# Half of the first Wq load issued from a second DMA queue

**The chip, the cores, the metric.** One core of one Trainium2 chip. The metric is the device time of one call in microseconds (us), lower is better.

## The reference

Four residual blocks on x of 2048 rows by 1024 columns in bf16: attention, feed-forward, attention, feed-forward, with the same weights in both rounds. Each block first normalises its input by rows. Only the first step of the first block matters here: the layer norm of the first 512 rows, and the Q projection of them.

```python
def _A_ref(x, wqkv, wo):              # x is normalised, wqkv is [1024, 3072]
    qkv = x @ wqkv                    # -> q, k, v, 32 heads of 32
    ...                               # 8 dilated positions (step 2) per row, softmax
    return o @ wo
x = x + _A_ref(_layernorm(x), A_wqkv, A_wo)
x = x + _B_ref(_layernorm(x), B_w1, B_b1, B_w2, B_b2)
...                                   # both once more
```

## The kernel before

The kernel works on groups of 512 rows (four tiles of 128 rows, x0 to x3 in the first group). `act`, `vec`, `pool` and `sp` wrap ScalarE, VectorE, GpSimd and SyncE; `.on = True` keeps the instructions of that engine in program order. All loads at the start are issued by SyncE: two x tiles, then 512 KB of Wq (two row blocks of 128 rows, of eight) in turn with the other x tiles.

```python
def load_wq_piece(wt, k):
    sp.dma_start(wt[:, k % (KD // 2):k % (KD // 2) + 2, :], wqkv_v[:, k:k + 2, 0:D])

load_x(0, 0, 2)                                   # x0, x1
wq_first = [wpool.tile([P, KD // 2, D], BF16, name="wt") for _ in range(2)]
for k in range(0, KD, 2):                         # KD = 8
    load_wq_piece(wq_first[k // (KD // 2)], k)
    if k < 4:
        load_x(0, 2 + k // 2, 3 + k // 2)         # x2, x3
...
act.activation(one[:], eps_t[:], ACT.Sqrt)        # brings in the Sqrt table early
```

Meanwhile TensorE runs 14 warm-up matmuls. VectorE takes the statistics of x0 and x1, ScalarE their square roots (`std`), VectorE normalises both; then TensorE transposes them and starts on Q, two row blocks of Wq at a time, for these two tiles. The transposes of x2 and x3 come in between.

```python
stats(0); stats(1)                                # bn_stats x2, bn_aggr; act: Sqrt -> std
xn0 = norm(0); xn1 = norm(1, (0, 2 * P, D))       # reciprocal, (x - mean) * rstd
transpose_on_pe(xn0, ...); transpose_on_pe(xn1, ...)
stats(2); stats(3)
for tt in range(2, 4):
    first_late.append((norm(tt), xa[0][:, tt, :, :]))
...
for kq in range(4):                               # two row blocks of Wq
    for c in range(7):
        first[c] = qkv_chunk(wq, c, xnT, first.get(c), kq * 2, (kq + 1) * 2, 0, 2)
        if (kq, c) in ((2, 3), (3, 4)):
            transpose_on_pe(*first_late.pop(0), ...)   # x2, then x3
```

The lines L92 and L117 of the profile are the helpers that record the operations and the matmuls; L211 (L213 to L218 in the variants) is the transpose.

## Time and profile before

| | before |
|---|---|
| median of 3 runs | 1230.35 us (1230.22 to 1230.75) |
| profiled span | 1228.4 us |
| TensorE busy | 1221.6 us, 99% |
| x0 landed / statistics of x1 start | 3.43 / 4.90 us |
| first weight load of Wq | 8.23 us |

After 8.23 us TensorE has just one gap, a short one, so a delay of that moment, or a new gap after it, can hardly be made up, and a load can win something only by bringing it forward. The prediction shows the lines of the start.

### The profile page before, as it was taken

The numbers are of one execution on the slowest core, as the hardware profiler recorded it, in microseconds if no ns is written. First come the engines' busy times: TensorE is split into PE (matmuls) and PEld (weight loads), VectorE is DVE, ScalarE is ACT, GpSimd is POOL, SyncE is SP. The second block draws the span as 40 slices with busy tenths as digits, with TensorE's granted clock in tenths as the row PEclk, the third lists the DMA queues.
The fourth block names the chain that finished last, engine by engine and source line by source line (L and its number), as shares of the span: only waits on it lengthen the run. The fifth ranks groups of instructions, "written<-read, shape, count | busy, mean of one in ns | idle before, by whom it ended". The sixth has DMA issues, their size and how long they took to land.

```text
span 1228.4 us, 13955 instructions
## 1 busy us (share of the span) xinstructions
PE 1221.6 (99%) x5720; PEld 632.7 (52%) x5770; DVE 861.5 (70%) x912; ACT 315.6 (26%) x497; POOL 120.9 (10%) x219
## 2 busy tenths in 40 slices
PE   9999999999999999999999999999999999999998
PEld 7666544456444564446544465444654444444444
DVE  7999896998898999375993759937599797011001
ACT  5343253014310233202431024410244001300310
POOL 2330025010101101100001000000000002000000
PEclk9999999999999999999999999999999999999999
DMA  9965674766638645856557565576664558446441
GB/s 302 290 206 164 176 233 151 202 178 199 219 128 245 188 150 166 239 170 175 161 158 230 172 171 181 157 216 201 171 200 147 186 194 209 149 159 194 156 135 52
DMA packets 223647, 226.64 MB, mean 185 GB/s; under 512 B 71824, under 2 KB 190752, under 8 KB 221536
## 3 DMA queue, kind: packets, MB, share of 16 engines
q1 hardware_dynamic: 214704, 208.69, 56.3%
q0 software_dynamic: 8880, 17.07, 4.2%
q8 instruction: 45, 0.74, 0.2%
q14 instruction: 18, 0.15, 0.0%
HBM read 189.01 MB, written 4.19 MB: 157 GB/s over the span
## 4 chain that ended last, share of the span: by engine, by line
PE 99%; DVE 0%; issue 0%; DMA 0%
PE acc L117 99%; DMA x<-in_A_x_dram 0%; DVE stats L92 0%; PE acc L211 0%; DVE xn L92 0%; DVE x L92 0%; DVE mv L92 0%; DVE rstd L92 0%
## 5 line engine op out<-in xcount | busy, mean ns | idle before, releaser
L117 PE MATMUL acc<-xnT,wt 128*128 128x512 bf16 (+1 forms) x3392 | 720.3, 375 | 0.1
L117 PEld LDWEIGHTS <-wt 128*128 128x128 bf16 x3392 | 400.8, 120 | 317.4
L117 PE MATMUL acc<-wt,hT 128*128 128x512 bf16 (+1 forms) x1780 | 386.0, 376 | 2.1
L117 PEld LDWEIGHTS <-hT 128*128 128x128 bf16 x1820 | 178.1, 98 | 209.0
L92 DVE TENSOR_TENSOR big<-big 128x1024 bf16<-128x1024 bf16 (+2 forms) x184 | 244.8, 1359 | 2.2
L92 ACT ACTIVATE hT<-acc,b1T 128x512 bf16<-128x512 f32 x224 | 152.1, 687 | 325.9 <-PE acc L117 325.8
L92 DVE TENSOR_TENSOR big<-qT,kT 128x4096 bf16<-128x4096 bf16 x64 | 143.8, 2283 | 36.3 <-ACT kT L92 35.9
L92 DVE TENSOR_TENSOR big<-abc,vT 128x4096 bf16<-128x4096 bf16 x64 | 144.6, 2284 | 11.0 <-DMA abc<-a 7.1
L92 DVE TENSOR_TENSOR tmp<-acc,b2bc 128x512 f32<-128x512 f32 x56 | 38.6, 689 | 159.8 <-PE acc L117 156.7
L92 ACT CAST qT<-acc 128x512 bf16<-128x512 f32 (+1 forms) x72 | 38.0, 543 | 276.8 <-PE acc L117 274.6
L117 PE MATMUL acc<-wt,oT 128*128 128x512 bf16 x440 | 97.6, 379 | 0.4
L92 DVE BATCH_NORM_STATS2 stats<-x 128x6 f32<-128x512 bf16 x116 | 77.4, 681 | 6.0 <-DMA x<-in_A_x_dram 5.0
L117 PEld LDWEIGHTS <-oT 128*128 128x128 bf16 x448 | 43.8, 98 | 53.0 <-issue 0.3
L92 DVE TENSOR_TENSOR x<-acc,big 128x512 bf16<-128x512 f32 (+1 forms) x9 | 5.7, 632 | 90.0 <-PE acc L117 90.0
L92 POOL TENSOR_TENSOR rstd<-mv,eps_t 128x1 f32<-128x1 f32 x54 | 16.7, 308 | 524.2 <-DVE mv L92 524.2
L92 ACT CAST vT<-acc 128x512 bf16<-128x512 f32 x64 | 37.4, 585 | 101.9 <-PE acc L117 101.9
L92 ACT CAST kT<-acc 128x512 bf16<-128x512 f32 x64 | 37.3, 584 | 64.5 <-PE acc L117 64.5
L92 DVE TENSOR_TENSOR x<-acc,x 128x512 bf16<-128x512 f32 x64 | 42.9, 670 | 5.1 <-PE acc L117 4.7
L92 DVE TENSOR_SCALAR xn<-x,mv,rstd 128x1024 bf16<-128x1024 bf16 (+2 forms) x53 | 28.5, 540 | 20.1 <-POOL rstd L92 19.9
L92 DVE TENSOR_TENSOR x<-tmp,x 128x512 bf16<-128x512 f32 x56 | 38.6, 689 | 1.4
L92 POOL DMA_DIRECT2D big<-big x24 | 13.3, 563 | 212.5 <-DVE big L92 212.5
L92 ACT ACT_TABLE_LOAD x17 | 21.8, 1283 | 38.9 <-DVE e L92 30.5
(62 smaller groups left out, 285.4 us busy)
## 6 DMA issues: line engine op xcount, KB each, us to landing
wt<-in_B_w_dram SPq DMA_DIRECT2D x56, 1024.0 KB, 5.6
wt<-in_B_w_dram SPq DMA_DIRECT2D x64, 896.0 KB, 4.8
wt<-in_A_wqkv_dram SPq DMA_DIRECT2D x46, 1024.0 KB, 5.6
wt<-in_A_wo_dram SPq DMA_DIRECT2D x16, 1024.0 KB, 5.0
abc<-a POOLq DMA_DIRECT2D x32, 256.0 KB, 4.6
big<-big POOLq DMA_DIRECT2D x24, 256.0 KB, 3.8
x<-in_A_x_dram SPq DMA_DIRECT2D x16, 256.0 KB, 7.1
out_dram<-x SPq DMA_DIRECT2D x31, 128.0 KB, 1.8
```

The costliest lines, as they stand in the source:

```text
L92: inst = f(*args, **kwargs)
L117: return pe(nc.tensor.matmul(*args, **kwargs))
```

## The change

The idea: ScalarE has little to do in the first microseconds and has a DMA queue of its own. Let it issue every second row block of the first Wq (1, 3, 5, 7), in pieces of 256 KB, while SyncE issues the others between the x tiles. Two issuers get the loads out sooner, and smaller pieces let the first matmul start on less.

```diff
-    def load_wq_piece(wt, k):
-        sp.dma_start(wt[:, k % (KD // 2):k % (KD // 2) + 2, :], wqkv_v[:, k:k + 2, 0:D])
+    def load_wq_piece(wt, k, engine):
+        engine.dma_start(wt[:, k % (KD // 2), :], wqkv_v[:, k, 0:D])
...
-        load_wq_piece(wq_first[k // (KD // 2)], k)
+        load_wq_piece(wq_first[k // (KD // 2)], k, sp)
...
+    act.on = True
     act.activation(one[:], eps_t[:], ACT.Sqrt)
+    act.on = True
+    for k in range(1, KD, 2):
+        load_wq_piece(wq_first[k // (KD // 2)], k, act)
+    act.on = False
```

## The prediction

> **What bounds the kernel now.** I first read the head of the page and its summary of the chain that ended last.
>
> ```profile
> span 1228.4 us, 13955 instructions
> PE 1221.6 (99%) x5720; PEld 632.7 (52%) x5770; DVE 861.5 (70%) x912; ACT 315.6 (26%) x497; POOL 120.9 (10%) x219
> PE 99%; DVE 0%; issue 0%; DMA 0%
> ```
>
> TensorE is busy for 1221.6 of 1228.4 us and is 99% of the chain. (The timed median, 1230.35 us, is 1.95 us above this span.) The change touches only loads issued in the first 10 us, so I next took the chain for the first 20 us (start, length, what ran):
>
> ```profile
> 0.74 2.69 DMA x<-in_A_x_dram
> 3.46 1.30 DVE stats L92 x2
> ...
> 6.44 0.55 DVE xn L92
> ...
> 7.10 0.74 DVE xn L92 x2
> ...
> 7.89 0.51 PE acc L211 x6
> 8.40 4.01 PE acc L117 x36
> 12.41 0.45 PE acc L211 x8
> 12.85 1.75 PE acc L117 x16
> 14.61 0.45 PE acc L211 x8
> 15.05 5.03 PE acc L117 x46
> ```
>
> No Wq load is in it. The end hangs on x0's landing (3.43 us), then on VectorE's statistics and normalising of tiles 0 and 1 up to 7.84, then on TensorE without a break. L211 are transposes, L117 the matmuls; before 7 us TensorE only runs warm-up matmuls. The timeline of the same stretch (start, length, engine, what, count) shows the work that could break that row:
>
> ```profile
> 4.90 1.23 DVE L92 BATCH_NORM_STATS2 stats<-x 128x6 f32<-128x512 bf16 x2
> 8.03 1.28 DVE L92 BATCH_NORM_STATS2 stats<-x 128x6 f32<-128x512 bf16 x2
> 8.23 3.94 PEld L117 LDWEIGHTS <-wt 128*128 128x128 bf16 x36
> 9.93 1.29 DVE L92 BATCH_NORM_STATS2 stats<-x 128x6 f32<-128x512 bf16 x2 [0.38 <-DMA x<-in_A_x_dram]
> 11.53 0.55 DVE L92 TENSOR_SCALAR xn<-x,mv,rstd 128x1024 bf16<-128x1024 bf16 x1
> 12.14 0.54 PEld L211 LDWEIGHTS <-xn 128*128 128x128 bf16 x8
> ```
>
> These rows are the statistics of x1, x2 and x3, the normalising of x2 and its transposes. The statistics of x3 waited 0.38 us for their DMA, and x2 is normalised after them: done at 11.53 + 0.55 = 12.08, and TensorE needs it at 12.14. Slack: 0.06 us.
>
> The last view is the table of stretches of 1 us; its last two columns are the DMA engines' busy share and GB/s:
>
> ```profile
> 2.00:3.00 1.00, 1.00 (x4) 0.30 (x2) 0.00 (x0) 0.23 (x2) 0.00 (x0) 1.00 0.96 274
> 4.00:5.00 1.00, 1.00 (x4) 0.41 (x3) 0.97 (x4) 0.00 (x0) 0.00 (x0) 1.00 1.02 233
> 6.00:7.00 1.00, 1.00 (x3) 0.15 (x1) 0.93 (x5) 0.29 (x1) 0.00 (x0) 1.00 1.05 387
> ```
>
> The engines are full from 2 us on, at 233 to 300 GB/s up to 6 us and 370 to 400 after it. Bytes arrive in a fixed stream, so what counts is their order.
>
> I checked order against arrival. Summing the stretches gives 0.32 MB moved by 3 us, 0.62 by 4, 0.85 by 5, 1.12 by 6, 1.50 by 7, 1.87 by 8, 2.25 by 9, 2.65 by 10, 3.05 by 11, 3.44 by 12. The DMA view of single issues gives the landings, as issue plus time to landing: x0 3.4, x1 about 4.3, Wq blocks 0-1 7.3 (1.66 + 5.6), x2 7.9 (2.13 + 5.8), blocks 2-3 9.2, x3 9.9 (3.11 + 6.8), blocks 4-5 11.2, blocks 6-7 12.6. In issue order each is complete in the byte count at 2.8, 3.7, 5.8, 6.5, 7.9, 8.6, 9.9 and 11.2 us. So a tile lands 0.6 us (the first two) or about 1.35 us (the others) after the stream has passed it. That rule carries the estimate below.
>
> When TensorE needs Wq: 36 weight loads in 3.94 us are 0.109 us each, 14 for two row blocks. Blocks 0-1 are needed at 8.23, 2-3 at 9.76, 4-5 at 11.29, and 6-7, after the transposes of x2, at about 13.3. Slacks before: 1.0, 0.5, 0.1 and 0.7 us. The start is loaded just in time.
>
> **What the Trainium skill says.** "DMA: Bandwidth & Descriptors", section "Issuing engines are not separate DMA queues": DMAs from scalar, sync or gpsimd run on the same 16 engines and interleave; a second issuer saves only sequencer time. The trace agrees as far as it goes: the engines are already 84 to 100% busy from SyncE's queue alone. The same page, "Queues, rings and completion order": SP and ACT own one queue row each, and every DMA engine takes turns between the rows by packets. The trace before has just one hardware queue carrying data, so it shows nothing of this. "Perfetto Trace Analysis", section "DMA Instruction — HWDGE (DVE, Sync)": the descriptor generator is locked by one sequencer at a time and the profiled length of an issue holds that wait. The first six of SyncE's issues take 0.40 to 0.47 us for either 256 or 512 KB, so ScalarE's issues may be stretched when both want it.
>
> **The change part by part.** The build order of the changed kernel leaves the work of TensorE, VectorE and GpSimd alone.
>
> Removed: nothing in bytes. Four loads of 512 KB become eight of 256 KB, four on each issuer.
>
> Added on ScalarE: four issues right after the Sqrt that ends at 2.24 us (2.04 + 0.20). At 0.45 us each that is 1.8 us, 3.6 if both issuers alternate for the generator. The fourth also waits for x0's landing at 3.43, because the build has only eight DMA semaphores. ScalarE's next work, the first std, started at 5.02 and is needed by VectorE at 6.30, after 0.29 us of run time. Issues that end by 4.1 to 5.9 us cost nothing.
>
> Moved on SyncE: through the same eight semaphores, x3's issue now waits for x1's landing (4.3 to 4.8 us, was issued at 3.11), block 4 for block 1, block 6 for block 0. These waits are mostly hidden behind a full stream.
>
> Moved in the stream: SyncE's row holds x0, x1, block 0, x2, block 2, x3, then 4 and 6; ScalarE's holds 1, 3, 5, 7. x0's first data came about 1 us after its issue, so ScalarE's row begins at about 3.25 us, with 0.40 MB gone. I let both rows share evenly from there and keep the old rate. A tile whose place in SyncE's row ends at s MB is then passed when 0.40 + 2 (s - 0.40) MB have moved, until ScalarE's 1.05 MB are out. x1 (0.52) lands at 4.8, needed at 4.90: just in time. Block 0 (0.79): 1.18 MB, 6.2 + 1.35 = 7.5, fine. x2 (1.05): 1.70 MB, 7.5 + 1.35 = 8.9, wanted at 8.03. Block 2 (1.31): 2.23 MB, 8.9 + 1.35 = 10.3, wanted at 9.76. x3 (1.57): all of ScalarE's row lies before it, 2.62 MB instead of 2.10, 9.9 + 1.35 = 11.3, was 9.91. Block 4: 11.9, wanted at 11.3.
>
> The stalls share one clock and do not add up: block 2 holds TensorE for 0.5 us, block 4 then for about 0.1, and x2's normalising, 2.15 us after the start of x3's statistics (9.93 to 12.08), ends at 13.4 instead of 12.08. TensorE would be at its transposes at 12.8, so the total loss is about 1.3 us. With TensorE full to the end, all of it reaches the end. This is the pessimistic sum: it takes the slow early rate and an even split. If ScalarE's issues come later, or two rows lift the 233 to 300 GB/s, x3 comes back to 10 us and the loss to 0. At 390 GB/s from 3.25 us on, 2.62 MB are passed at 3.25 + 2.22 / 0.39 = 8.9 rather than 9.9, and x3 lands at 10.3: a loss of 0.3 us. I take 0.75 us, near the middle of 0.3 and 1.3: 1231.1 us.
>
> **The rivals.** First, faster streaming through finer pieces and two rows. For it: the slow stretch coincides with SyncE's long run of issues, and 256 KB pieces release TensorE a block at a time. Against it: the engines are counted full there, and no Wq wait is on the chain, so a perfect stream wins only the 0.06 us and perhaps some of the 0.3 us gap inside the first transposes. It would give 1230.1 to 1230.4. Second, ScalarE held up: if its issues block past 6 us, the first std delays normalising, and every 0.1 us passes to the end; at 1 us an issue the fourth ends at 6.3 and costs about 0.3 us, 1230.7 alone. Third, x1 crowded out by ScalarE's first block: it has 0.5 us of room, and I expect it to use that; beyond it, each tenth counts in full. All three rivals and a bad x3 together would make some 1232.3.
>
> **Range and chances.** Low: no loss and 0.25 us of run-to-run spread (the three runs before span 0.5), 1230.1. High: the full x3 loss with 0.6 us of the second or third rival, 1232.3. A step of 2% is 24.6 us, longer than the whole stretch touched: faster 0.5%, within 2% 98.5%, slower 1%.
>
> **What would show it.** Right: in the profile after, a second hardware queue or ScalarE issues of 256 KB from about 2.24 us; x3's statistics starting at 10.3 to 11.3 us with a longer DMA wait; the transposes of x2 starting at 12.5 to 13.5 behind a TensorE gap; the matmul row shifted by the same amount to the end. Wrong: those transposes still at 12.14 with the same span (the rivals of a better stream), or a first real transpose later than 7.05 (ScalarE or x1). An effect over 2 us, or any difference arising after 20 us, would show that I have misread what bounds the start.

## The result

| | before | changed |
|---|---|---|
| median | 1230.30 us (5 runs, 1230.14 to 1230.75) | 1230.67 us (5 runs, 1230.62 to 1231.06) |
| profiled span | 1228.4 us | 1228.9 us |
| statistics of x1 start | 4.90 us | 5.30 us |
| first weight load of Wq | 8.23 us | 8.68 us |

The ratio is 1.0003, with a 95% interval of 0.999 to 1.0017: the same at 2%, and by the interval not even clear of nothing. What makes 0.4 us readable at all is that the profiles show where TensorE falls behind and catches up, and that the same pattern came back in a second set of runs (e6 below).

The head of the page of the changed kernel and, from its table of DMA queues (packets, MB, share of 16 engines), the new hardware queue:

```profile
span 1228.9 us, 14009 instructions
PE 1224.0 (100%) x5770; PEld 632.7 (51%) x5770; DVE 861.9 (70%) x912; ACT 315.8 (26%) x497; POOL 124.4 (10%) x219
...
q10 hardware_dynamic: 576, 1.05, 0.2%
```

The second queue is there: 1.05 MB, which is the four blocks. TensorE's 2.4 us more of busy time is a matter of records: 5770 matmuls against 5720 before, where 50 records were missing (the weight loads are 5770 in both).

The chain that ended last, of the changed kernel's first 20 us (start, length, what):

```profile
1.19 4.08 DMA x<-in_A_x_dram
...
5.30 1.30 DVE stats L92 x2
...
7.54 0.75 DVE xn L92 x2
...
8.34 0.51 PE acc L216 x6
8.85 3.99 PE acc L117 x36
...
15.48 4.59 PE acc L117 x42
```

Set this beside the chain before. There it began with x0, issued at 0.74; here it begins with x1, issued at 1.19 and 4.08 us under way. Before, x1 needed 3.1 us, was there at 4.3 and was not on the chain. From x1 on, the two chains have the same steps of the same length, 0.44 to 0.45 us apart (7.10 and 7.54, 7.89 and 8.34, 8.40 and 8.85). At the last row shown the distance is 0.43 us.

Later it changes twice. TensorE's weight loads at 124 us, of the kernel before and then of the changed one:

```profile
124.36 2.68 PEld L117 LDWEIGHTS <-oT 128*128 128x128 bf16 x13 [0.28 <-issue]
```

```profile
123.55 3.33 PEld L117 LDWEIGHTS <-oT 128*128 128x128 bf16 x16
```

The gap of the kernel before is missing in the changed one, which is 0.43 us behind up to this place and 0.27 us behind after it. That distance holds to VectorE's last operation, in the same order:

```profile
1225.38 0.42 DVE L92 TENSOR_TENSOR x<-acc,big 128x256 bf16<-128x256 f32 x1 [0.34 <-PE acc L117]
```

```profile
1225.65 0.42 DVE L92 TENSOR_TENSOR x<-acc,big 128x256 bf16<-128x256 f32 x1 [0.34 <-PE acc L117]
```

From the end of this operation to the end of the span there are 2.56 us before and 2.81 us changed. The trace has the instructions that the views leave out: at the end SyncE waits for the DMA semaphores in a fixed order, about 0.06 us apart. The loads and stores of SyncE and ScalarE take eight semaphores in turn, so four more loads at the start give the last store another one. Before, its wait is the eighth of nine (at 1227.39 us, one more follows); changed, it is the fourth (at 1227.68 us, five more follow). So the profiled span, which grew by 0.52 us (1228.36 to 1228.88), owes 0.27 us to the late start and 0.25 us to there being four more loads, whichever queue issues them.

The timeline of the same stretch (start, length, engine, what, count, in brackets the idle time before and what ended it):

```profile
0.74 1.28 ACT L92 ACT_TABLE_LOAD   x1 [0.74 <-PEq L671]
0.91 1.34 ACTq L92 DMA_DIRECT2D wt<-in_A_wqkv_dram  x3
2.03 0.20 ACT L92 ACTIVATE one<-eps_t 128x1 f32<-128x1 f32 x1
3.51 0.34 ACTq L92 DMA_DIRECT2D wt<-in_A_wqkv_dram  x1
5.30 1.28 DVE L92 BATCH_NORM_STATS2 stats<-x 128x6 f32<-128x512 bf16 x2 [0.26 <-DMA x<-in_A_x_dram]
8.68 3.92 PEld L117 LDWEIGHTS <-wt 128*128 128x128 bf16 x36
10.04 1.29 DVE L92 BATCH_NORM_STATS2 stats<-x 128x6 f32<-128x512 bf16 x2
11.63 0.55 DVE L92 TENSOR_SCALAR xn<-x,mv,rstd 128x1024 bf16<-128x1024 bf16 x1
12.56 0.54 PEld L216 LDWEIGHTS <-xn 128*128 128x128 bf16 x8
```

Three readings. ScalarE issued its first three loads at 0.91 us, while the table load was running and before the Sqrt that stands ahead of them in its program. The statistics of x1 waited 0.26 us for their DMA; the rest of their 0.40 us of delay is that those of x0 began 0.05 us later, and that before they had overlapped the aggregation of x0 (4.78 to 4.99) by 0.09 us. And the statistics of x3 (10.04) have no wait in brackets any more: x2 is normalised by 12.18 and TensorE wants it at 12.56, a slack of 0.38 us where it had 0.06.

The table of stretches (the last two columns are the DMA engines' busy share and GB/s):

```profile
4.00:5.00 1.00, 1.00 (x4) 0.41 (x3) 0.96 (x3) 0.00 (x0) 0.00 (x0) 1.00 1.03 391
5.00:6.00 1.00, 1.00 (x4) 0.30 (x2) 0.74 (x3) 0.29 (x1) 0.00 (x0) 1.00 1.02 371
```

From 4 us on the stream ran at 369 to 410 GB/s, where it had 233 and 266 in the two stretches from 4 to 6 us before. So the later tiles came sooner than the old stream would have brought them, by the DMA view of single issues: x2 at 8.4, block 2 at 9.3, x3 at 10.0, block 4 at 10.7. Block 1 had landed at 4.6, 0.7 us ahead of x1, though TensorE had no use for it before 8.7. The same view, asked for stretches, counts both queues: up to 2.5 us the second had moved nothing and the first 0.16 MB; from 2.5 to 5 us the second moved 0.47 MB and the first 0.38 MB. They took nearly even turns while x1 was on its way.

### The profile page after: what moved, and what is told of

Same layout as the page of the kernel before. It is cut to its first block, busy times and chain, and to the rows that moved or that the text cites. A ratio compares the mean times of both kernels' runs of the same rounds, so it can differ in the third digit from the quotient of the medians.

```text
span 1228.9 us, 14009 instructions
## 1 busy us (share of the span) xinstructions
PE 1224.0 (100%) x5770; PEld 632.7 (51%) x5770; DVE 861.9 (70%) x912; ACT 315.8 (26%) x497; POOL 124.4 (10%) x219
## 3 DMA queue, kind: packets, MB, share of 16 engines
q10 hardware_dynamic: 576, 1.05, 0.2%
## 4 chain that ended last, share of the span: by engine, by line
PE 99%; DMA 0%; DVE 0%; SPq 0%; issue 0%
PE acc L117 99%; DMA x<-in_A_x_dram 0%; PE acc L216 0%; DVE stats L92 0%; DVE xn L92 0%; DVE x L92 0%; SPq L92 0%; DVE mv L92 0%; DVE rstd L92 0%
```

## The experiments

**Theory.** ScalarE's queue goes out at 0.9 us and takes its turns on the DMA engines while x1 is still in SyncE's queue. x1, which VectorE wants 0.5 us after it used to land, comes 1 us later. **Rivals.** The smaller pieces, which use up the eight DMA semaphores sooner, delay x1; ScalarE itself is held up by its issues; or the 0.4 us are noise.

All variants computed the right result. Times are medians in us beside those of the kernel before. Kernels are compared only within the same rounds. The third column is x1's time from issue (about 1.19) to landing, the fourth the wait of x1's statistics for it, the fifth the start of the first Wq weight load, the sixth what TensorE waited for Wq or x tiles after that, the last the time from the end of VectorE's last operation to the end of the span.

| run | time / before | x1 us | wait | first Wq | later waits of TensorE | end |
|---|---|---|---|---|---|---|
| before, profile | | 3.1 | 0 | 8.23 | 0 | 2.56 |
| changed, profile | 1230.67 / 1230.30 | 4.1 | 0.26 | 8.68 | 0 | 2.81 |
| e1_fine_sp | 1230.42 / 1230.47 | 3.1 | 0 | 8.42 | 0 | 2.80 |
| e2_act_after_x0 | 1231.00 / 1230.47 | 3.0 | 0 | 8.65 | 0 | 2.82 |
| e3_two_queues_512 | 1230.84 / 1230.47 | 4.3 | 0.43 | 8.93 | 0.1 | 2.56 |
| e4_x1_from_act | 1231.26 / 1230.47 | 3.8 (issued at 0.74) | 0 | 9.14 | 0 | 2.80 |
| e5_three_after_x0 | 1231.15 / 1230.36 | 3.0 | 0 | 8.25 | 1.15 (block 1), 0.60 at 60 us | 2.81 |
| e6_after_again | 1230.71 / 1230.36 | 4.0 | 0.24 | 8.64 | 0 | 2.80 |
| e7_before_again | 1230.19 / 1230.36 | 3.0 | 0 | 8.33 | 0 | 2.56 |
| e8_x0_halves | 1230.38 / 1230.36 | 3.1 | 0 | 8.41 | 0.35 (block 4) | 2.49 |
| e9_half_block | 1230.45 / 1230.18 | 3.6 | 0 | 8.45 | 0 | 2.74 |
| e10_one_block | 1230.64 / 1230.18 | 4.1 | 0 | 8.78 | 0 | 2.83 |
| e11_late_blocks | 1231.68 / 1230.18 | 3.0 | 0 | 8.40 | 0.9 + 0.3 + 1.0 | 2.56 |

The last column goes with the number of loads: 2.80 to 2.83 us in every run with four more than before, 2.56 in those with as many (e3, e7, e11), 2.74 with five more (e9), 2.49 with one more (e8).

### e1: the pieces without the queue

```diff
         load_wq_piece(wq_first[k // (KD // 2)], k, sp)
+        load_wq_piece(wq_first[k // (KD // 2)], k + 1, sp)
...
-    for k in range(1, KD, 2):
-        load_wq_piece(wq_first[k // (KD // 2)], k, act)
```

> All eight 256 KB blocks of the first Wq from SyncE's queue, in the order 0 to 7 with the x tiles where they were; no issue from ScalarE. Theory (ScalarE's queue row takes its turns while x1 is still in SyncE's row, and x1 lands about 1 us late): without the second row x1 lands at 4.2 to 4.4 us after start as before, its statistics start at 4.90, the first real transpose at 7.05, and the time is that of the kernel before within 0.1 us. The stream between 4 and 6 us stays slow (230 to 270 GB/s), if the second row is what sped it up. Rival (the finer pieces, with the eight semaphores they use up sooner, delay x1 and speed the stream): statistics of x1 at 5.3, first transpose at 7.5, 0.4 us slower than before, and 370 GB/s or more from 4 us on. Second rival (the speed comes from the pieces, the delay from the row): on time and fast stream.

The time is that of the kernel before, and x1 took 3.1 us. From its timeline, the statistics of x1:

```profile
5.09 1.23 DVE L92 BATCH_NORM_STATS2 stats<-x 128x6 f32<-128x512 bf16 x2
```

They follow those of x0 without a wait; that they start at 5.09, not 4.90, is because x0 itself landed 0.19 us later in this profile. So the pieces and their semaphores do not delay x1. They do lengthen the end, to 2.80 us, which the median does not show: 0.25 us is of the size of the noise here. The stream was 268 and 326 GB/s from 4 to 6 us: between the two kernels, so my clean expectation of slow or fast was not met.

### e2 and e5: the second queue held until x0 has landed

```diff
+    act.activation(one[:], x[0][:, 0:1], ACT.Identity)
     for k in range(1, KD, 2):          # e5: range(1, KD - 2, 2), and block 7 from sp
         load_wq_piece(wq_first[k // (KD // 2)], k, act)
```

> The changed kernel, with one small ScalarE activation that reads a column of x0 put ahead of ScalarE's four issues, so that they go out only when x0 has landed, at about 3.5 us instead of 0.91. Theory (x1 is crowded by ScalarE's early blocks): x1 is nearly through by then; statistics of x1 at 4.9, first transpose at 7.05 to 7.1, time within 0.15 us of the kernel before, so 0.3 to 0.45 us under the changed kernel. Rival (x1 is late because of the semaphores, or because two issuers share the descriptor generator whenever they issue): x1 stays at 5.3 and the loss stays. What I do not know is whether block 1, issued at 3.5, is there by 8.23; by the one-row stream it lands at about 7.5.

ScalarE's timeline in e2, and then two rows of its chain:

```profile
3.65 2.64 ACTq L92 DMA_DIRECT2D wt<-in_A_wqkv_dram  x4
6.33 0.48 ACT L92 ACTIVATE std<-mv,eps_t 128x1 f32<-128x1 f32 x2 [2.50 <-DVE stats L92]
```

```profile
1.67 4.27 DMA wt<-in_A_wqkv_dram
...
5.95 0.34 ACTq L92
```

The brackets name VectorE, but it had aggregated x0 by 5.09 us; the chain shows the issue that ended just before.

x1 was cured (3.0 us, no wait), which is the theory's half. But the time was 0.53 us above before (of the 0.77 us in its profile, 0.26 us are the longer end). At the start, the fourth issue waited for block 0, because their semaphore was the same, until 5.95 us, and ScalarE could not begin the first `std` until 6.33, after VectorE wanted it. That is the second rival of the prediction, brought in by my edit. It doesn't happen in the changed kernel, whose fourth issue is over at 3.85. e5 takes this wait away.

> As e2 (ScalarE's issues held until x0 has landed), but block 7 goes from SyncE, so that ScalarE has no issue left that waits for another load's landing (in e2 the fourth waited until 5.95 us and held the first std to 6.33). Theory (in e2 x1 was cured and only ScalarE's blocked queue cost time): statistics of x1 not waited for, first std right after its statistics (about 0.3 us after those of x0 end), first transpose 3.6 to 3.7 us after the statistics of x0 start, as in the kernel before; time within 0.15 us of before. Rival (any second-row traffic in the first 8 us costs something): 0.3 us or more over before.

The first half again held: statistics of x1 at 4.92 without a wait, first Wq weight load at 8.25. Then this, from TensorE's weight loads:

```profile
8.25 0.14 PEld L117 LDWEIGHTS <-wt 128*128 128x128 bf16 x1
9.54 3.81 PEld L117 LDWEIGHTS <-wt 128*128 128x128 bf16 x35 [1.15 <-DMA wt<-in_A_wqkv_dram]
```

One weight load of block 0, then 1.15 us of waiting for block 1, which had been held back too long. So my expectation of a time as before failed (1231.15 against 1230.36, and scattered over 1230.33 to 1231.93; the profile is of the slowest of the five runs), and for a new reason: the same block that crowds x1 when it is early is late when it is not. By the DMA view the second queue moved nothing before 6.2 us in e2 and e5, 2.6 to 2.7 us after its first issue, where the changed kernel's began 1.6 us after. So they show that x1 is on time when the second queue moves nothing beside it; they show no cure.

### e3: the queue without the pieces

```diff
-        load_wq_piece(wq_first[k // (KD // 2)], k)       # 512 KB
+        if k % 4 == 0:
+            load_wq_piece(wq_first[k // (KD // 2)], k, sp)
...
+    for k in range(2, KD, 4):
+        load_wq_piece(wq_first[k // (KD // 2)], k, act)
```

> The four 512 KB loads of the kernel before, blocks 0-1 and 4-5 from SyncE, 2-3 and 6-7 from ScalarE. Theory (the second row crowds x1, whatever the piece): statistics of x1 at 5.2 to 5.5, first transpose at 7.4 to 7.6, 0.3 to 0.5 us slower than before; and if the second row is what speeds the stream, 370 GB/s or more between 4 and 6 us. Rival (finer pieces and their semaphores): x1 at 4.9, time as before, stream slow between 4 and 6 us.

x1 took 4.3 us, its statistics waited 0.43 us, and the time rose by 0.37 us as in the changed kernel. The stream ran at 404 and 356 GB/s from 4 to 6 us. With e1 this is the answer on both counts: an early second queue delays x1 whatever the size of the pieces, and the pieces alone do not. The first transpose was at 7.74, 0.14 us beyond what I expected; the statistics of x1, at 5.55, and the 356 GB/s missed their ranges by less. Since e3 has no more loads than the kernel before, its end is the same 2.56 us, and the 0.67 us by which its profiled span is longer all come from the start.

### e4: x1 itself on the second queue

```diff
-    load_x(0, 0, 2)
+    load_x(0, 0, 1)
+    act.dma_start(x[1][:], x_in[P:2 * P, :])
```

> The changed kernel with x1 as ScalarE's first issue, ahead of its blocks, and x0 the only tile ahead of block 0 in SyncE's row. Theory (a tile is delayed by what shares the turns with it while it is in its row): x1 has no Wq data beside it but block 0 at the end, so it lands at about 4.2 and its statistics are not waited for (start 4.9 or right after those of x0); x0 now shares its turns with x1 and may land up to 0.4 us later, which would pass straight to the end. I expect x0 at 3.4 to 3.8, first transpose at 7.05 to 7.45, time between the kernel before and the changed one. If x0 is not touched, the time is that of before. Rival (x1 late for another reason than what shares the stream): x1's statistics at 5.3 as in the changed kernel.

x1 was not waited for; x0 was. The chain of e4:

```profile
0.74 3.60 DMA x<-in_A_x_dram
...
4.37 1.30 DVE stats L92 x2
```

x0 took 3.60 us instead of 2.69, more than twice the delay I allowed, and this run is slower than the changed kernel (0.79 us over before, 0.66 without the run at the lower clock). So the tile that shares its turns pays, whichever it is. x0 is the worse one to choose, since nothing stands between its landing and the first statistics.

### e6 and e7: both kernels again

No edit: the two kernels as they are.

> The changed kernel once more, to see how far one profile can be trusted. Theory: statistics of x1 waited for again, 0.1 to 0.6 us, starting at 5.1 to 5.6; ScalarE's first issue again at 0.9, during the table load; stream again above 350 GB/s from 4 us on; 0.2 to 0.5 us slower than before. Rival (the delay of x1 in the first profile was chance): x1 on time and no difference.

> The kernel before once more, as the measure of noise. Theory: no wait for x1, x0 landing at 3.4 to 3.7, the stream again at 230 to 330 GB/s between 4 and 6 us; ratio 1.0000 within 0.0001. Rival (differences of 0.2 to 0.4 us between kernels are noise): it differs from before by as much as the changed kernel does.

Both came out as the theory says. The changed kernel: x1 4.0 us, wait 0.24, 0.35 us above before, 377 and 334 GB/s from 4 to 6 us. The kernel before: no wait for x1, and an even slower stream (211 and 164 GB/s). The kernel before against itself differed by 0.17 us in the medians (ratio 0.9998), so 0.35 us is about twice the noise; the intervals of all three include 1. The time alone would not decide it. That the same wait appears in both profiles of the changed kernel and in neither of the kernel before does.

### e8: only x0 on two queues

```diff
-    load_x(0, 0, 2)
+    sp.dma_start(x[0][:, 0:HALF], x_in[0:P, 0:HALF])
+    act.dma_start(x[0][:, HALF:D], x_in[0:P, HALF:D])
+    load_x(0, 1, 2)
```

> The kernel before, with x0 alone changed: its left 512 columns from SyncE and its right 512 from ScalarE, both as the first issue of their queue; everything else from SyncE as before. Theory (the end hangs on the moment x0's statistics can start, nothing else in these loads): the statistics of the left half start when 128 KB are there, so 0.1 to 0.3 us earlier, if the right half follows within 0.68 us, the length of one statistics instruction; the time falls by as much, to about 1230.1 to 1230.3, under both kernels. Rival (issue and landing latency, not bytes, set x0's arrival; and e4 showed that two rows delay x0): start at 3.4 or later, no gain or a small loss.

The rival won. The halves took 2.9 and 3.1 us from issue to landing, where the whole tile, but for e4 and e10, takes 2.7 to 2.9; statistics began at 3.63, and there was no gain (1230.38 against 1230.36).

### e9 and e10: how much of the second queue it takes

```diff
+    act.dma_start(wq_first[0][:, 1, 0:HALF], wqkv_v[:, 1, 0:HALF])   # e9; its right half from sp
+    load_wq_piece(wq_first[0], 1, act)                               # e10, in its place
```

(All other blocks from SyncE in 256 KB pieces, as in e1.)

> A dose of the second row: only the left half of block 1 (128 KB) from ScalarE, at 0.9 us; all else in 256 KB pieces from SyncE as in e1. Theory (x1 waits for the bytes that take turns with it): at most 0.13 MB more go before x1, about 0.35 us of stream at the 330 to 390 GB/s of this stretch; x1 lands 3.3 to 3.5 us after its issue (3.0 to 3.1 without a second row, 4.0 to 4.1 in the changed kernel), so at 4.5 to 4.7, before its statistics want it at about 4.9; no wait, time as before. Rival (the delay comes with any second-row traffic, not with its bytes): 4.0 us and a wait as in the changed kernel.

> As e9 with the whole of block 1 (256 KB) from ScalarE, one issue. Theory: up to 0.26 MB before x1, 0.65 to 0.75 us; x1 lands 3.7 to 3.9 us after its issue, at 4.9 to 5.1; a wait of 0 to 0.2 us, time 0 to 0.2 us over before. The rest of the changed kernel's delay (4.0 to 4.1) then comes from the second block, 3. Rival: 4.0 or more already here, or 3.1 and no effect (then it takes all of ScalarE's queue).

The DMA view of x1's issue, in e9 and then in e10 (its last number is us from issue to landing):

```profile
x<-in_A_x_dram SPq DMA_DIRECT2D x1, 256.0 KB, 3.6
```

```profile
x<-in_A_x_dram SPq DMA_DIRECT2D x1, 256.0 KB, 4.1
```

With 0, 128 and 256 KB on the second queue, x1 took 3.1, 3.6 and 4.1 us; with 1 MB (the changed kernel) 4.1 and 4.0. So half a block gave about half the delay, and one block all of it, each in a single profile. I had under-sized it: 0.35 us expected for the half block, 0.5 measured; 0.65 to 0.75 for the block, 1.0 measured. In e10 x0 was late too (3.24 us after its issue), so x1's statistics queued behind x0's rather than waiting for x1. The late first Wq loads of e9 and e10 (0.22 and 0.55 us after that of before) thus follow from x0, and the times, 0.27 and 0.46 us over before, also hold the longer end: they say nothing of x1's cost.

### e11: only the late blocks on the second queue

```diff
+        if k < 4:
             load_wq_piece(wq_first[k // (KD // 2)], k, sp)          # 512 KB, as before
...
+    act.activation(one[:], x[0][:, 0:1], ACT.Identity)
+    for k in range(4, KD, 2):
+        load_wq_piece(wq_first[k // (KD // 2)], k, act)
```

> The version that the runs so far point to for a use of the second queue: 512 KB loads as in the kernel before, blocks 0-1 and 2-3 from SyncE, and only the late ones, 4-5 and 6-7, from ScalarE, held until x0 has landed. Theory (the end hangs on x0, x1 and VectorE; no load later than x1 has anything to win): x1 not waited for, no TensorE wait for a Wq block if 4-5, issued at 3.6 instead of 3.62, keeps its place; first matmul 4.7 to 4.8 us after the start of x0's statistics as before; time as before within 0.15 us, no gain. Risk: the blocks 4-5 and 6-7 now share turns with blocks 2-3 and x3, which had the row to themselves; if x3 or 2-3 come 0.3 us later or more, TensorE waits and it is slower by that. Rival (two queues stream faster and that is worth time): 0.2 us or more under before.

The risk that I named happened, five times as large as the 0.3 us that I gave it as a threshold. VectorE's and TensorE's lines:

```profile
10.86 1.52 PEld L117 LDWEIGHTS <-wt 128*128 128x128 bf16 x14 [0.94 <-DMA wt<-in_A_wqkv_dram]
12.28 1.28 DVE L92 BATCH_NORM_STATS2 stats<-x 128x6 f32<-128x512 bf16 x2 [1.69 <-DMA x<-in_A_x_dram]
...
14.47 0.45 PEld L217 LDWEIGHTS <-xn 128*128 128x128 bf16 x8 [0.97 <-DVE xn L92]
```

The profile is of the slowest of the four runs. x3 landed at 12.25, 9.1 us after an issue that was no later than before; its statistics waited 1.69 us, the transposes of x2 then held TensorE for 0.97 us, and blocks 2-3 had held it for 0.94 us before that. The run is the slowest of all, 1.50 us over before. The stream was at 240, 190 and 209 GB/s from 4 to 7 us, the lowest over that stretch, and by the DMA view all of it was the first queue's: the second, issued from 3.67 us, moved nothing before 8.0.

## Why the prediction was right or wrong

The time was within the range, 0.43 us under the point, and "the same" was right. The main step that carried the point was not what happened.

**What bounds the kernel: right for the start, incomplete for the rest.** The delay of the first Wq weight load lasted to 124 us as the prediction says (0.45 us, then 0.43). There 0.16 us of it came back, and at the end 0.25 us were added by the four more loads. The span less the start of the first Wq load looks like a constant, 1228.4 - 8.23 = 1220.17 before and 1228.9 - 8.68 = 1220.22 changed, but that is luck: the two nearly cancel. The prediction called any difference after 20 us a sign that it had misread the bound; these two it had not foreseen. e3, the second queue without more loads, is the cleaner case: 0.70 us late at the first Wq load, 0.67 us longer in the span.

**When ScalarE issues: wrong.** This is the step that failed first: "Added on ScalarE: four issues right after the Sqrt that ends at 2.24 us". They went out at 0.91. The Trainium skill's "Perfetto Trace Analysis", section "DVE / Act Engine Instruction (TENSOR_ADD, Activation, etc)", says that an engine's sequencer pushes an instruction into a wait queue and then is ready for the next. I had cited its neighbour on DMA instructions and not this one. The trace agrees with it: the issues at 0.91 do not wait for a table load that ends at 2.02. In e2 the trace has a separate semaphore instruction of ScalarE, at 3.56 us, that held the queue until x0 had landed; the first issue, at 3.65, then started before the activation of 3.63 to 3.83 had ended.

**When x1 lands: a term mis-sized by that step, and the term that decided.** I had ScalarE's data begin at 3.25 us, when 0.40 MB had gone, and x1 land at 4.8, "just in time". It landed at 5.28, and the first transpose came at 7.49, later than the 7.05 that the prediction names as a sign of being wrong. By the same rule, landing 0.6 us after the stream has passed, x1 was passed at 4.68, when the stretches sum to 0.88 MB; 2 x 0.52 - 0.88 puts the start of the sharing at 0.16 MB. The queue counts above bear this out: the second queue's data began at 2.5 us, with 0.16 MB moved, and the split was near even from there. The doses fit less well: by the same rule and their own stretches I work out 3.5 us from issue to landing for e9 and 3.7 for e10, and they took 3.6 and 4.1. So the crowding and the near-even turns are shown, but bytes alone do not give the landing in e10. This was my third rival, "x1 crowded out", and e1, e3 and e9 with e10 show it: no second queue, no delay; a second queue with large pieces, the same delay; half a block, half the delay.

**The stall through x3: did not happen.** The sum said x2 at 8.9, block 2 at 10.3, x3 at 11.3, block 4 at 11.9, for a loss of 1.3 us, softened to 0.75. They came at 8.4, 9.3, 10.0 and 10.7, and TensorE, itself 0.45 us late by then, waited for none. The assumption "keep the old rate" failed: 391 and 371 GB/s from 4 to 6 us instead of 233 and 266. I had named that way out, and put its effect on x3 at 10.3. The mechanism is not false: in e11, where the second queue brought its 1 MB later and the stream stayed slow, x3 came at 12.25, and TensorE waited as the sum describes. There the stretches sum to 1.55 MB by 8.0 us, when the second queue began, and x3 ends at 2.10 MB in its row, so even turns pass it after 1.10 MB more. By the stretches I estimate that for 10.8 us, and with 1.35 us to land x3 comes at 12.1. In the changed kernel it was bought off by the faster stream.

**The second rival, ScalarE held up:** it did not occur in the change (the last issue ended at 3.85, against the 4.1 to 5.9 that I called harmless, and three issues beside SyncE's took 1.34 us, no longer apiece than SyncE's alone) but did in e2.

**SyncE's waits for semaphores: right.** x3 was issued at 5.29, on x1's landing, and its wait was hidden behind the full stream: its statistics did not wait.

**No gain to be had: right.** The first rival, a faster stream, came true and won nothing, because no load after x1 was on the chain.

So the number was near by luck: a stall through x3, booked with 0.75 us, did not come, and in its place stood 0.27 us from x1, booked as zero, and 0.25 us at the end that I had not thought of.

**What stays open.** Why the stream was fast from 4 us on. It ran at 334 to 420 GB/s from 4 to 6 us in the six profiles with ScalarE's first Wq data issued at about 0.9 to 1.3 us (changed, e3, e4, e6, e9, e10, even with 128 KB in e9), and at 164 to 326 in the others. A second queue at work in that stretch is not needed (in e9 and e10 it had moved all its data by 4 and 4.3 us), and an early issue by ScalarE of any kind is not enough (e8 had 128 KB of x0). e2, e5 and e11 do not test it: their second queue moved nothing before 6.2 to 8.0 us, though issued from 3.6 us on, and why it began so late no run tells. Nor is it known what TensorE's gap at 124 us is. Nor do the runs tell why x0 was late in e10 (3.24 us) and not in the changed kernel, which issues the same load first: these are single profiles.

## What to carry to other kernels

With the DMA engines full, the second queue was no second road here: what it carried took turns with what VectorE was waiting for, and an urgent tile in one queue paid for a block in the other that was not needed yet. Before moving a load to another queue, ask which landing starts the chain, and keep the other queue silent until that landing; then check that the moved load is not late itself, as e5 and e11 were. One queue in the order of need was as good as anything tried here, and within noise the best. And follow a delay through to the end of the profile before you call the difference in time its price: here half of the longer span came from elsewhere.

## What the Trainium skill lacked or had wrong

- "DMA: Bandwidth & Descriptors", "Issuing engines are not separate DMA queues", says that a second issuer only saves sequencer time. It also changes the order of arrival: x1 took 3.1 us from issue to landing with one queue, 3.6 with 128 KB and 4.1 with 256 KB on the other. The section on queues and rings has the turn-taking from which this follows, but not this consequence.
- No page that I read says how early loads stream at a kernel's start. Here the DMA engines counted as 86 to 107% busy at 164 to 266 GB/s from 4 to 6 us in the two profiles of the kernel before, and as 93 to 104% busy at 334 to 391 GB/s in the two of the changed one.
- "Perfetto Trace Analysis" was right where I overlooked it (a sequencer is free once an instruction is queued): issues at 0.91 us beside a table load until 2.02.
- No page that I read says that the number of earlier loads can change how long a program takes to end: 2.56 us after VectorE's last operation before, 2.80 to 2.83 us in every run with four more loads.
